# Two interleaved halves: another walk through the same elements in the gate operations of VectorE

## The chip, the core and the metric

The kernel runs on one core of one Trainium2 chip. The time is device microseconds (us) of one execution, from launch to end. A core has TensorE (PE, matrix products), VectorE (DVE), ScalarE (ACT), GpSimd (POOL) and SyncE (SP, which here issues the transfers, DMAs). Each engine works through its own list of instructions in a fixed order and waits at semaphores for the others.

## The reference

Two blocks follow each other. The first is a gated recurrence with complex decays, for 4 batches, 8 heads, 768 tokens and a head size of 48; the second is a two-layer network with a PReLU on 3072 tokens of 384 features, with 2048 hidden features.

```python
mag = np.sqrt(a_re * a_re + a_im * a_im)
scale = np.minimum(mag, 0.999) / (mag + 1e-06)
a_re_n, a_im_n = (a_re * scale, a_im * scale)
for t in range(S):
    ar, ai = (a_re_n[:, :, t, :, None], a_im_n[:, :, t, :, None])
    new_re = ar * S_re - ai * S_im
    new_im = ar * S_im + ai * S_re
    kv = np.einsum('bhd,bhe->bhde', k[:, :, t], v[:, :, t])
    S_re, S_im = (new_re + kv, new_im)
    y[:, :, t] = np.einsum('bhd,bhde->bhe', q[:, :, t], S_re)

x = y.transpose(0, 2, 1, 3).reshape(B * S, H * D)
h = x @ w_in
g = np.maximum(h, 0.0) + alpha * np.minimum(h, 0.0)
return g @ w_out
```

Everything is float32 on the chip.

## The kernel before, in words

**Stages.** The work is cut into tasks that are Python generators. `gates` (nine tasks, one per batch and group of C chunks of 128 tokens: one task with C=1, one with C=2, seven with C=3) loads the decays a_re and a_im, normalises them, forms products of the unit complex numbers along time and writes two scratch tensors to DRAM: `decs` (products of magnitudes) and `phs` (products of phases). `unit` (24 tasks, one per batch and chunk) loads q, k, v and those scratch tensors as the tiles KQ, V and VL, PP and T, and does the attention part of a chunk by levels: DVE multiplies KQ by phases (L742, L744) and by decays (L797), ACT copies parts of it (L820, L836), PE multiplies (L759), and masks, states and sums follow. `features` and `outputs` are the network: PE multiplies tokens by `w_in` (L978) into one of two PSUM buffers `ps_h`, ACT and DVE form the PReLU (L985, L987), PE multiplies by `w_out` (L997). For the last three groups of tokens `late_features` and `late_outputs` do the same with fewer products (L1097, L1172).

**Order.** A string, `ORDER`, says which task makes its next step; each step issues a few instructions. This one order fixes the list of every engine, so an instruction of `gates` on DVE stands between instructions of `unit` and of the network, and those behind it wait for it.

**The gate operations.** A gate task holds six areas of N = 3·128·C elements per partition (384, 768 or 1152) in one tile `gate`: x, c, f, d, e, y. For all tasks but the first, these DVE operations go over one whole area, in place: c+d (L269), e·c (L279), (e-3)·d (L281), c·d (L289), and x·d and y·d (L363, twice). The first task has its own lines (L305 to L323), in halves of 192. In all nine tasks `decays` forms the capped magnitude from c and f and writes it to `dec`, in rows of 128 with gaps of 128 (L380); a tree of products follows (L396). The chain of unit numbers uses `U`, which holds re and im as (m, n, i), that is the eight places within a block as four pairs, then the block n, then the place within the pair; products of neighbours go over it (L416, L418). The last step multiplies each block's numbers by the block's starting phase (L507, four per task) and sums (L510), and `phs` is written from there. The short recurrence over runs (L416 and L418 with 12 and 6 elements) is on DVE; other operations of up to 80 elements in the later gate tasks are on POOL.

In all of these the engines go through an area in the order in which it lies in memory, apart from L396, L416, L418 and L510, which take or leave pairs or every second element.

Of the kernel before, what the change touches and what calls it, by code (L numbers as in the profile page):

```python
# [14 lines left out]
ALU = mybir.AluOpType  # L15
# [3 lines left out]
P = 128  # L19
MAG_CAP = 0.999  # L20
# [4 lines left out]
GATE_SCALE = 2.0 ** 16  # L25
# [79 lines left out]
def kernel(  # L105
# [123 lines left out]
    def gates(g, b, c0, c1):  # L229
        C = c1 - c0  # L230
        n = C * P
        N = NK * n
        first, last = c0 == 0, c1 == NCH
        TT = nc.vector.tensor_tensor
        STT = nc.vector.scalar_tensor_tensor
# [11 lines left out]
        flat = flat_[:, 0:6 * N]  # L247
        G = flat.rearrange("p (r n) -> p r n", r=6)
        x, c, f, d, e, y = [G[:, i] for i in range(6)]
        dec = flat[:, 3 * N:5 * N].rearrange("p (m s) -> p m s", s=TL)  # L250
        for z, src in ((x, a_re), (y, a_im)):
            z = z.rearrange("p (t s) -> p t s", t=NK)
# [5 lines left out]
        if g:  # L258
            t = yield ACT(N, t)
            if last:  # L260
                ends_ = G[:, 0:6:5].rearrange("p r (t s) -> p r t s", t=NK)[:, :, :, n - 1]
                nc.scalar.activation(ends_, ident[:, 0:2 * NK].rearrange("p (r t) -> p r t", r=2), AF.Copy, scale=0.0)
            nc.scalar.activation(x, x, AF.Identity, scale=1.5, bias=bias_tiny)
            yield ACT(N)
            nc.scalar.activation(c, x, AF.Square, scale=GATE_SCALE)
            t = yield ACT(N, t)
            nc.scalar.activation(d, y, AF.Square, scale=1.5 * GATE_SCALE)
            t = yield DVE(N, t)
            TT(out=c, in0=c, in1=d, op=ALU.add)  # L269

            t = yield ACT(N, t)
            nc.scalar.activation(d, c, AF.Abs_reciprocal_sqrt)
            t = yield ACT(N, t)
            nc.scalar.activation(e, d, AF.Square)

            te = yield ACT(N, t)
            nc.scalar.activation(f, e, AF.Abs_reciprocal_sqrt)
            t = yield DVE(N, te)
            TT(out=e, in0=e, in1=c, op=ALU.mult)  # L279
            t = yield DVE(N, t)  # L280
            STT(out=d, in0=e, scalar=3.0, in1=d, op0=ALU.subtract, op1=ALU.mult)  # L281
            tf = yield ACT(N)
            nc.scalar.activation(f, f, AF.Square, scale=ONE / (1.5 * GATE_SCALE * MAG_EPS), bias=bias_one)
            tf = yield ACT(N)
            nc.scalar.activation(f, f, AF.Abs_reciprocal_sqrt)
            tf = yield ACT(N)
            nc.scalar.activation(f, f, AF.Identity, scale=ONE / 2.0, bias=bias_half)
            ts = yield DVE(N, t)
            TT(out=c, in0=c, in1=d, op=ALU.mult)  # L289
            ts = yield ACT(N, ts)  # L290
            nc.scalar.activation(c, c, AF.Copy, scale=1.0 / (1.5 * GATE_SCALE))
        else:
            parts = [[z[:, N // 2 * h:N // 2 * (h + 1)] for z in (x, c, f, d, e, y)] for h in range(2)]
            ready, tf, ts, txs = [None, None], [None, None], [None, None], [None, None]

            def enter(h):
                x, c, f, d, e, y = parts[h]
                yield ACT(N // 2, tx)
                nc.scalar.activation(x, x, AF.Identity, scale=1.5, bias=bias_tiny)
                yield ACT(N // 2)  # L300
                nc.scalar.activation(c, x, AF.Square, scale=GATE_SCALE)
                r = yield ACT(N // 2, t)
                nc.scalar.activation(d, y, AF.Square, scale=1.5 * GATE_SCALE)
                ready[h] = yield DVE(N // 2, r)
                TT(out=c, in0=c, in1=d, op=ALU.add)  # L305

            def root(h):
                x, c, f, d, e, y = parts[h]
                r = yield ACT(N // 2, ready[h])
                nc.scalar.activation(d, c, AF.Abs_reciprocal_sqrt)  # L310
                r = yield ACT(N // 2)
                nc.scalar.activation(e, d, AF.Square)
                r = yield ACT(N // 2)
                nc.scalar.activation(f, e, AF.Abs_reciprocal_sqrt)
                yield DVE(N // 2, r)
                TT(out=e, in0=e, in1=c, op=ALU.mult)
                yield DVE(N // 2)
                STT(out=d, in0=e, scalar=3.0, in1=d, op0=ALU.subtract, op1=ALU.mult)
                for p, w in ((y, -0.75), (x, -0.5)):
                    txs[h] = yield DVE(N // 2)  # L320
                    STT(out=p, in0=p, scalar=w * GATE_SCALE, in1=d, op0=ALU.mult, op1=ALU.mult)
                ts[h] = yield DVE(N // 2)
                TT(out=c, in0=c, in1=d, op=ALU.mult)  # L323

            for h in range(2):
                yield from enter(h)
            for h in range(2):
                yield from root(h)

        L = 8  # L330
        nb = N // L
        U = G[:, 0:3] if C > 2 else flat_[:, 6 * N:9 * N].rearrange("p (r n) -> p r n", r=3)
        U5 = U.rearrange("p r (m n i) -> p r m n i", m=L // 2, i=2)
# [7 lines left out]
        def by_place(z):  # L341
            return z.rearrange("p (n m i) -> p m n i", m=L // 2, i=2)

        def unit_numbers(*after):

            if not g:
                for h in range(2):
                    part = slice(nb // 2 * h, nb // 2 * (h + 1))
                    for o, p, by in ((2, y, 1.0), (0, y, -1.0), (1, x, 1.0)):
                        tu = yield ACT(N // 2, txs[h])  # L350
                        nc.scalar.activation(U5[:, o, :, part], by_place(p)[:, :, part], AF.Copy, scale=by)
                return tu
            for o, p in ((2, y), (1, x)):
                tu = yield ACT(N, tx, *after)
                nc.scalar.copy(U5[:, o], by_place(p))
            tu = yield ACT(N)
            nc.scalar.activation(U[:, 0], U[:, 2], AF.Copy, scale=-1.0)
            return tu

        if g:  # L360
            for p, w in ((x, -0.5), (y, -0.75)):
                tx = yield DVE(N, t)
                STT(out=p, in0=p, scalar=w * GATE_SCALE, in1=d, op0=ALU.mult, op1=ALU.mult)  # L363
        else:
            tu = yield from unit_numbers()
            tf = yield ACT(N)
            nc.scalar.activation(f, f, AF.Square, scale=ONE / (1.5 * GATE_SCALE * MAG_EPS), bias=bias_one)
            tf = yield ACT(N)
            nc.scalar.activation(f, f, AF.Abs_reciprocal_sqrt)
            tf = yield ACT(N)  # L370
            nc.scalar.activation(f, f, AF.Identity, scale=ONE / 2.0, bias=bias_half)
            ts = yield ACT(N, ts[1])
            nc.scalar.activation(c, c, AF.Copy, scale=1.0 / (1.5 * GATE_SCALE))
# [3 lines left out]
        def decays():  # L377

            t = yield DVE(N, ts, tf)
            STT(out=dec[:, :, 0:P], in0=c.rearrange("p (m s) -> p m s", s=P), scalar=-2.0 * MAG_CAP,  # L380
                in1=f.rearrange("p (m s) -> p m s", s=P), op0=ALU.max, op1=ALU.mult)
            yield POOL(2 * NK * C, t)
            nc.gpsimd.memset(dec[:, :, TL - 2:TL], 0.0)
            return t

        t = yield from decays()
        if C > 2:
            tu = yield from unit_numbers(t)
        f = y
        at = 0  # L390
        while at < TL - 4:
            m = (TL - at) // 2
# [28 lines left out]
        def turned(z, o):  # L421

            return z[:, 1 + o::-1][:, 0:2]
# [12 lines left out]
        off3 = y[:, 5 * nb:8 * nb].rearrange("p (r n) -> p r n", r=3)  # L436
# [37 lines left out]
        m = f[:, 0:2 * k].rearrange("p (a l n) -> p a l n", a=2, l=Rn - 1)  # L474
        for o in range(2):
            yield tiny(2 * k, t)
            tiny_engine.tensor_tensor(out=m, in0=blk[:, :, 0:Rn - 1],  # L477
               in1=turned(runs, o).unsqueeze(2).to_broadcast([P, 2, Rn - 1, rows]), op=ALU.mult)
# [24 lines left out]
        m = G[:, 3:5].rearrange("p a (m n i) -> p a m n i", m=L // 2, i=2)  # L503
        for o, p in enumerate((x, y)):
            for a in range(2):
                yield DVE(N, t, sent)
                TT(out=m[:, a], in0=U5[:, 1 + a], in1=turned(off3, o)[:, a].unsqueeze(1).unsqueeze(3).to_broadcast(  # L507
                    [P, L // 2, nb, 2]), op=ALU.mult)
            ts = yield DVE(N)
            TT(out=by_place(p), in0=m[:, 0], in1=m[:, 1], op=ALU.add)  # L510
            used = yield DMA(N / 2, ts)
            nc.sync.dma_start(phs[:, o, 1:n + 1].rearrange("(t p) s -> p t s", p=P), p.rearrange("p (t s) -> p t s", t=NK))
# [748 lines left out]
```

## Time and profile before

| what | value |
|---|---|
| median of three runs | 835.8 us (831.9 to 836.94) |
| the profiled execution | 834.89 us |
| its span, first to last instruction | 833.2 us |
| mean granted TensorE clock | 0.963 |
| PE busy | 685.4 us (82%) |
| DVE busy | 691.2 us (83%) in 1151 instructions |
| ACT busy | 502.7 us (60%) |
| POOL busy | 249.5 us (30%) |
| DMA moved | 130.98 MB |

The profile is of one execution. A row of the groups of instructions names the line, engine, operation, tiles and shapes; then the number of instructions, their busy time in us, the mean of one in ns, and the time that the engine sat idle just before them. A busy engine is not an engine at its peak: TensorE's ends are modelled. Shares are of the span. Times inside the profile are counted from the start of the span.

### The profile page before, as it was taken

Reading aid. Unit: us, or ns where it says so; the run is one execution under the profiler, and the core shown is the slowest. Engines: PE = TensorE matmul, PEld = TensorE weight load, DVE = VectorE, ACT = ScalarE, POOL = GpSimd, SP = SyncE. Lnnn points to the kernel's source line nnn. Section 1 sums busy time; section 2 is a strip of 40 time slices with the busy share of each in tenths; the row PEclk is TensorE's granted clock in tenths of the full one; section 3 lists DMA queues with packets and bytes.
Section 4 is the critical chain, followed back from the end, with each engine's and each line's share of the span. In section 5 each row is a group of like instructions: output and inputs, shape, how many; then the busy total and the mean of one; then the engine's idle time right before and its main releaser. Section 6 shows DMA issues by size and latency. Waiting matters only on the chain.

```text
span 833.2 us, 27790 instructions
## 1 busy us (share of the span) xinstructions
PE 685.4 (82%) x11680; PEld 542.5 (65%) x11680; DVE 691.2 (83%) x1151; ACT 502.7 (60%) x1243; POOL 249.5 (30%) x341
## 2 busy tenths in 40 slices
PE   0001316859999999899999999999999999999997
PEld 0001315646777667667777777776777777899997
DVE  6978989999999889899998999997887585556574
ACT  8848777557657767776876589554755645311121
POOL 7457454651503110233043121402300000323432
PEclk9999755979999999999999999999999999999999
DMA  7794885696678559547975779678476631201000
GB/s 210 224 274 121 251 233 163 194 217 162 154 226 195 149 145 261 152 123 214 247 177 156 233 165 208 179 193 189 96 204 146 158 90 36 61 2 39 1 20 20
DMA packets 186597, 130.98 MB, mean 157 GB/s; under 512 B 74728, under 2 KB 176872, under 8 KB 186088
## 3 DMA queue, kind: packets, MB, share of 16 engines
q1 hardware_dynamic: 186472, 129.20, 58.5%
q8 instruction: 92, 1.51, 0.8%
q14 instruction: 33, 0.27, 0.1%
HBM read 100.82 MB, written 35.71 MB: 164 GB/s over the span
## 4 chain that ended last, share of the span: by engine, by line
PE 62%; DMA 13%; DVE 11%; SPq 4%; ACT 4%; POOL 4%; issue 2%; DVEq 0%; ACTq 0%; POOLq 0%
PE ps_o L997 18%; PE ps_h L978 16%; PE ps_m L1172 6%; PE ps_lv L759 4%; PE ps_h L1097 3%; PE ps_y L1097 3%; PE ps_y L900 3%; PE ps_kv L880 2%; DVE KQ L797 2%; PE ps_y L930 2%; DVE gate L507 2%; DMA T<-decs 2%; DMA ysc<-T 2%; DMA VL<-in_v_dram 1%; DMA g_sb<-in_w_out_dram 1%
## 5 line engine op out<-in xcount | busy, mean ns | idle before, releaser
L978 PE MATMUL ps_h<-xT,w_in_sb 128*128 128x256 f32 (+1 forms) x960 | 227.8, 369 | 2.8 <-DMA xT<-ysc 1.8
L997 PE MATMUL ps_o<-w_out_sb,g_sb 128*128 128x384 f32 x576 | 224.7, 505 | 5.2 <-DVE g_sb L987 5.0
L978 PEld LDWEIGHTS ps_h<-xT,w_in_sb 128*128 128x128 f32 x960 | 173.0, 196 | 54.9 <-issue 3.2
L797 DVE TENSOR_TENSOR KQ<-KQ,T 96x1024 f32<-96x1024 f32 x120 | 148.8, 1241 | 25.4 <-PE ps_lv L759 18.1
L997 PEld LDWEIGHTS ps_o<-w_out_sb,g_sb 128*128 128x128 f32 x576 | 101.8, 191 | 45.6 <-DVE g_sb L987 7.6
L985 ACT ACTIVATE g_sb<-ps_h 128x256 f32<-128x256 f32 (+1 forms) x160 | 58.0, 362 | 84.7 <-PE ps_h L978 84.1
L759 PE MATMUL ps_lv<-WQ 96*32 96x32 f32 x2304 | 34.9, 204 | 81.7 <-DVE WQ L742 63.0
L416 POOL TENSOR_TENSOR gate<-gate 128x72 f32<-128x72 f32 (+1 forms) x56 | 43.1, 770 | 177.6 <-ACT gate L446 166.1
L759 PEld LDWEIGHTS ps_lv<-WQ 96*32 96x32 f32 x2304 | 26.6, 116 | 101.2 <-DVE WQ L742 63.4
L987 DVE SCALAR_TENSOR_TENSOR g_sb<-g_sb,al,ps_h 128x256 f32<-128x256 f32 (+1 forms) x160 | 71.4, 446 | 20.6 <-ACT g_sb L985 20.4
L1160 POOL TENSOR_TENSOR sums<-g_sb 128x128 f32<-128x128 f32 x48 | 21.9, 476 | 182.0 <-DMA VL<-in_v_dram 109.0
L916 ACT ACTIVATE St<-St,T 96x48 f32<-96x48 f32 x288 | 68.7, 325 | 6.1 <-DVE St L918 6.1
L820 ACT COPY WQ<-KQ 96x1024 f32<-96x1024 f32 x48 | 50.0, 1042 | 23.2 <-DVE KQ L797 23.2
L596 POOL TENSOR_SCALAR top<-top 128x768 f32<-128x768 f32 x16 | 42.6, 2668 | 28.4 <-ACT top L588 26.1
L900 PE MATMUL ps_y<-A,VL 64*48 64x64 f32 x2304 | 42.2, 222 | 8.3 <-issue 6.6
L477 POOL TENSOR_TENSOR gate<-gate,runs 128x252 f32<-128x252 f32 (+1 forms) x16 | 21.0, 1311 | 86.4 <-ACT runs L446 60.5
L507 DVE TENSOR_TENSOR gate<-gate 128x1152 f32<-128x1152 f32 (+2 forms) x36 | 44.3, 1263 | 2.9 <-POOL gate L492 2.7
L416 DVE TENSOR_TENSOR gate<-gate 128x576 f32<-128x576 f32 (+3 forms) x70 | 45.3, 647 | 1.3 <-ACT gate L446 0.4
L900 PEld LDWEIGHTS ps_y<-A,VL 64*48 64x48 f32 x2304 | 39.3, 123 | 10.4 <-issue 9.6
L836 ACT COPY W<-KQ 96x512 f32<-96x512 f32 x48 | 30.8, 642 | 23.7 <-DVE KQ L797 17.4
L759 PE MATMUL ps_lv<-KQ,W 96*32 96x32 f32 x1536 | 24.6, 205 | 24.3 <-ACT W L836 24.0
L773 ACT ACTIVATE A<-ps_lv,columns 128x64 f32<-128x64 f32 x144 | 37.7, 338 | 9.5 <-PE ps_lv L759 9.1
(169 smaller groups left out, 1365.3 us busy)
## 6 DMA issues: line engine op xcount, KB each, us to landing
T<-decs SPq DMA_DIRECT2D x48, 384.0 KB
PP<-phs SPq DMA_DIRECT2D x24, 387.0 KB
KQ<-in_q_dram SPq DMA_DIRECT2D x48, 192.0 KB
decs<-gate SPq DMA_DIRECT2D x7, 1152.0 KB
phs<-gate SPq DMA_DIRECT2D x14, 576.0 KB
KQ<-in_k_dram SPq DMA_DIRECT2D x40, 192.0 KB
vsc<-in_v_dram SPq DMA_DIRECT2D x48, 144.0 KB
VL<-vsc SPq DMA_DIRECT2D x48, 144.0 KB
```

The costliest lines, as they stand in the source:

```text
L416: on(4 * k).tensor_tensor(out=m, in0=w[:, 1::-1].unsqueeze(2).to_broadcast([P, 2, 2, k]), in1=pairs_of(u), op=ALU.mult)
L507: TT(out=m[:, a], in0=U5[:, 1 + a], in1=turned(off3, o)[:, a].unsqueeze(1).unsqueeze(3).to_broadcast([P, L // 2, nb, 2]), op=ALU.mult)
L759: nc.tensor.matmul(t[64 * i + j:64 * i + j + HC // 2, p], lhsT=keys(n, g), rhs=queries(n, g), start=True, stop=True)
L797: nc.vector.tensor_tensor(out=x, in0=x if x0 is None else x0, in1=m, op=ALU.mult)
L820: nc.scalar.copy(z.rearrange("p i n t -> p i (n t)").rearrange("p i (m h) -> p m i h", h=h), bass.AP(tensor=KQ.tensor, offset=KQ.offset + ...
L900: nc.tensor.matmul(o, lhsT=Vp[h][64 * i:64 * i + 64, s, e_ * D:(e_ + 1) * D], rhs=a, start=False, stop=False)
L916: nc.scalar.activation(St[:, n], before[:, n], AF.Copy, scale=T[0:D2, n, TL - 4 + s:TL - 3 + s])
L978: nc.tensor.matmul(p, lhsT=w_in_sb[:, f // 2, kk, f % 2 * P:(f % 2 + 1) * P], rhs=x_of[m][:, kk], start=(kk == 0), stop=(kk == NK - 1))
L985: nc.scalar.activation(gt, p, AF.Relu, scale=-1.0)
L987: nc.vector.scalar_tensor_tensor(out=gt, in0=gt, scalar=al_1[:, f:f + 1], in1=p, op0=ALU.mult, op1=ALU.add)
L997: nc.tensor.matmul(sums[0], lhsT=gt[:, c * P:(c + 1) * P], rhs=w_out_sb[:, f], start=(f == 0), stop=(f == NF - 1))
L1097: nc.tensor.matmul(o, lhsT=lhs, rhs=rhs, start=(at in (0, 5)), stop=(at in (4, 8)))
```

## The change

A helper reads an area of N elements as two halves and walks them in turn: element 0, element N/2, element 1, element N/2+1, and so on. It is put on all operands of L269, L279, L281, L289 and L363. In `decays` (L380) the walk goes across the 3·C rows of 128 first and along a row second. In L507 the block n is now the outer loop and the place of the pair the inner one; the two elements of a pair stay neighbours. What is computed and where it is stored stay as they are, the number of instructions too, and so does the order on every engine.

```diff
+        def strides(z):
+            return z.rearrange("p (a b) -> p b a", a=2)
+
...
             t = yield DVE(N, t)
-            TT(out=c, in0=c, in1=d, op=ALU.add)
+            TT(out=strides(c), in0=strides(c), in1=strides(d), op=ALU.add)
...
             t = yield DVE(N, te)
-            TT(out=e, in0=e, in1=c, op=ALU.mult)
+            TT(out=strides(e), in0=strides(e), in1=strides(c), op=ALU.mult)
             t = yield DVE(N, t)
-            STT(out=d, in0=e, scalar=3.0, in1=d, op0=ALU.subtract, op1=ALU.mult)
+            STT(out=strides(d), in0=strides(e), scalar=3.0, in1=strides(d), op0=ALU.subtract, op1=ALU.mult)
...
             ts = yield DVE(N, t)
-            TT(out=c, in0=c, in1=d, op=ALU.mult)
+            TT(out=strides(c), in0=strides(c), in1=strides(d), op=ALU.mult)
...
                 tx = yield DVE(N, t)
-                STT(out=p, in0=p, scalar=w * GATE_SCALE, in1=d, op0=ALU.mult, op1=ALU.mult)
+                STT(out=strides(p), in0=strides(p), scalar=w * GATE_SCALE, in1=strides(d), op0=ALU.mult, op1=ALU.mult)
...
             t = yield DVE(N, ts, tf)
-            STT(out=dec[:, :, 0:P], in0=c.rearrange("p (m s) -> p m s", s=P), scalar=-2.0 * MAG_CAP,
-                in1=f.rearrange("p (m s) -> p m s", s=P), op0=ALU.max, op1=ALU.mult)
+            STT(out=dec[:, :, 0:P].rearrange("p m s -> p s m"), in0=c.rearrange("p (m s) -> p s m", s=P), scalar=-2.0 * MAG_CAP,
+                in1=f.rearrange("p (m s) -> p s m", s=P), op0=ALU.max, op1=ALU.mult)
...
                 yield DVE(N, t, sent)
-                TT(out=m[:, a], in0=U5[:, 1 + a], in1=turned(off3, o)[:, a].unsqueeze(1).unsqueeze(3).to_broadcast(
-                    [P, L // 2, nb, 2]), op=ALU.mult)
+                TT(out=m[:, a].rearrange("p m n i -> p n m i"), in0=U5[:, 1 + a].rearrange("p m n i -> p n m i"),
+                   in1=turned(off3, o)[:, a].unsqueeze(2).unsqueeze(3).to_broadcast([P, nb, L // 2, 2]), op=ALU.mult)
```

## The prediction, made before the changed kernel ran

> **What bounds the kernel now.** I read the slices of the page first, then busy time by stretch, then the waits of PE and DVE, then single rows of DVE and ACT.
>
> In the slices (each digit is the busy share of 1/40 of the span, 20.8 us, in tenths):
>
> ```profile
> PE   0001316859999999899999999999999999999997
> DVE  6978989999999889899998999997887585556574
> ```
>
> The reader is to see two stages. Until about 190 us PE is half empty, and the chain of waits runs through transfers, POOL and DVE. From then on PE is full, and until about 600 us DVE is nearly full beside it.
>
> The same by stretches around the gate tasks. The columns are the stretch, its length, then busy us of PE, PE's weight loads, DVE, ACT and POOL, the granted clock, the DMA share and GB/s:
>
> ```profile
> 12.00:50.00 38.00, 0.00 (x0) 0.00 (x0) 35.09 (x89) 26.85 (x42) 16.74 (x17) 1.00 0.74 231
> 50.00:100.00 50.00, 12.42 (x396) 10.55 (x396) 41.62 (x56) 37.36 (x53) 34.76 (x29) 0.95 0.71 205
> 100.00:128.00 28.00, 5.55 (x140) 4.72 (x140) 23.17 (x26) 18.22 (x24) 14.70 (x15) 0.50 0.94 255
> ...
> 260.00:300.00 40.00, 37.96 (x642) 28.04 (x635) 35.18 (x52) 30.05 (x78) 13.41 (x22) 0.96 0.56 138
> ...
> 330.00:370.00 40.00, 36.14 (x724) 26.61 (x723) 37.06 (x58) 30.23 (x79) 10.73 (x15) 1.00 0.61 157
> ...
> 408.00:440.00 32.00, 30.79 (x651) 23.29 (x650) 30.18 (x38) 26.67 (x69) 10.36 (x15) 1.00 0.79 194
> ...
> 484.00:514.00 30.00, 30.00 (x588) 22.66 (x590) 28.52 (x40) 25.77 (x70) 8.71 (x15) 1.00 0.76 179
> ```
>
> DVE has 38.00 - 35.09 = 2.9 us to spare in the first of these, then 8.4, 4.8, 4.8, 2.9, 1.8 and 1.5. In the waits of 200 to 514 us, PE waits for nothing in particular for more than a few us, and most of DVE's idle time there is put down to PE (ps_lv) or to ACT behind PE (g_sb). Two engines that are this full hand work to each other through two ps_h buffers: a delay of DVE is soon one of PE, and PE has no gap in which to make it up.
>
> **The change, part by part.** The built lists of instructions of the two kernels agree on every engine in number and order; only access patterns differ, L269 for instance being 384x2 instead of 768. So nothing is removed, added or moved, no queue is passed, no transfer and no wait is new. What can change is the duration of 57 DVE operations that now take each element from another place than the one before, and of the 36 of L507.
>
> Elements per partition that hop: six operations (L269, L279, L281, L289, twice L363) in seven tasks of 1152 and one of 768 make 6 × (7 × 1152 + 768) = 52,992. L380 adds 7 × 1152 + 768 + 384 = 9,216. Together 62,208.
>
> What a hop costs, the trace of before doesn't show for a long DVE operation. The nearest rows, here of DVE and ACT (the number after the bar's busy time is the mean of one in ns):
>
> ```profile
> L363 DVE SCALAR_TENSOR_TENSOR gate<-gate 128x1152 f32<-128x1152 f32 x14 | 19.0, 1368 | 0.0
> L510 DVE TENSOR_TENSOR gate<-gate 128x1152 f32<-128x1152 f32 x14 | 19.0, 1355 | 0.2
> L744 DVE TENSOR_TENSOR KQ<-KQ,PP 96x1024 f32<-96x1024 f32 x24 | 30.0, 1249 | 0.1
> L416 DVE TENSOR_TENSOR gate<-run,runs 128x12 f32<-128x12 f32 x48 | 8.2, 171 | 0.8
> L396 DVE TENSOR_TENSOR gate<-gate 128x12 f32<-128x12 f32 x1 | 0.2, 171 | 0.0
> L480 DVE TENSOR_TENSOR gate<-gate 128x42 f32<-128x42 f32 x1 | 0.2, 236 | 0.0
> L488 DVE TENSOR_TENSOR gate<-gate 128x48 f32<-128x48 f32 x1 | 0.2, 208 | 0.0
> L444 ACT COPY gate<-gate 128x288 f32<-128x288 f32 x7 | 5.0, 710 | 4.3 <-DVE gate L418 4.3
> L486 ACT ACTIVATE gate<-gate 128x288 f32<-128x288 f32 x7 | 3.1, 440 | 6.7 <-POOL gate L480 6.7
> ```
>
> - No cost: L744 steps 8 bytes on all three operands and L510 writes pairs with gaps between them; both go at the rate of L363, which is contiguous (1249 for 1024 and 1368 for 1152 differ by 0.93 ns per element). L416 on 12 elements reads in steps of some 28 bytes and takes the 171 ns of L396; 12 elements would show only 10 ns.
> - A cost: L480 writes 42 single elements 32 bytes apart. L488 writes 48 neighbours in 208 ns; at about 1.04 ns each (1368 - 171 over 1152 - 12 is 1.05) 42 would take 202, so each hop cost (236 - 202) / 42 = 0.81 ns. One sample, with POOL beside it. On ACT, L444 writes single elements 72 bytes apart and L486 as many neighbours: (710 - 440) / 288 = 0.94 ns.
>
> The bounds are thus 0 (the 28-byte reads) and, if reads and writes each pay as a write does here, 2 × 0.85 = 1.7 ns; below 0 nothing in these rows points. I take 0.85, between the DVE row and the ACT row and nearer to the first: the changed operations write single elements 2304 bytes apart (L380: 1024), which is nearest to L480. An operation of 1152 goes from 1360 to 1360 + 0.98 us = 2.34 us; DVE gains 62,208 × 0.85 ns = 52.9 us.
>
> The Trainium skill, page "Vector Engine (DVE) Microarchitecture Reference", section "Measured stream behaviour on trn2", speaks against the change: a port keeps its rate only in runs of two or more adjacent words, and with all three operands hopping it lists 1.98 ns per column against 1.054. By that an estimate of 0.93 × 62,208 = 57.6 us would stand for the 52.9. For words 8 bytes apart L744 does not bear the rule out in that form.
>
> L507 I cost at nothing: its pairs stay together on both long operands, as in L510, and only the repeated phase is read in another order.
>
> **What of it shows at the end.** A task of 1152 adds 6.85 us to DVE, the task of 768 4.6, the first 0.3. Lower end: each stretch uses all the idle time that it has. Then 4.9 - 2.9 = 2.0 remain in 12 to 50 us, nothing in 50 to 100, 2.0 in 100 to 128, 1.7 around the task of 182 to 213 (5.2 us idle in 170 to 260), 2.0 in 260 to 300, 3.9 in 330 to 370, 5.0 in 408 to 440, 5.4 in 484 to 514: 22 us. Upper end: all 52.9. Against the lower end speaks that DVE's waits are for PE and ACT, which come later themselves when DVE does, and that POOL, on the chain from 49 to 63 us, is held up beside DVE's operations of two operands:
>
> ```profile
> 52.44 0.29 POOL L416 TENSOR_TENSOR gate<-gate 128x48 f32<-128x48 f32 x1
> ...
> 54.04 2.50 POOL L416 TENSOR_TENSOR gate<-gate 128x48 f32<-128x48 f32 x1
> ```
>
> (DVE ran L744 and L269 back to back then.) Against the upper end speaks the second ps_h buffer, with which PE runs on for a group of some 2 us, and the transfers that carry the chain from 99 to 127 us. I take the middle, 37.5 us. The profiled execution is 834.9 us (span 833.2, 1.7 around it), 0.9 below the median of 835.8: 834.9 + 37.5 = **872 us**.
>
> **Rivals.**
> 1. The halves cost nothing because two alternating streams are each still sequential and both places are kept at hand; only L380, with nine rows in turn, pays. DVE gains 9,216 × 0.85 = 7.8 us, and by the same share of the way between the ends (0.7) 5.5 us show: 840. For it: the reads of L416 at no cost; against: L480 and L444 write regular steps too, and pay. The same section of the Trainium skill reports one stream alternating between two regions at the full read rate, for an operation with one source; no run here shows that yet.
> 2. Not slower: no hop costs anything at such lengths, because an operation over 1152 elements has its next ones fetched well ahead; L480's 34 ns are then POOL's doing and ACT's price is ACT's own. DVE's rows stay at 1350 to 1390 and the time is that of before, 832 to 838. It decides if the hop's price is under 0.15 ns, where the 9 us that it adds to DVE vanish in its 32 us of idle time in the stretches above. A faster end would need the interleaved operations to free POOL; no row shows such a thing.
> 3. Reads and writes both pay: 1.7 ns. DVE gains 106 us, more than all its idle time from 12 to 514 us (43 us), so between 63 and 106 show: about 920.
> 4. The change does nothing because the walk is straightened out again when the kernel is built; the 384x2 in the built list speaks against that. It would look like 2 and is counted there.
>
> **How the numbers follow.** Forecast 0.70: 834.9 plus 22 to 53, that is 857 to 888, and with a price of 0.65 to 1.0 ns 852 to 897. Rival 1 0.12 (836 to 846), rivals 2 and 4 0.08, rival 3 0.08, anything faster 0.02. The range of 840 to 897 holds the forecast's 0.70 and most of rival 1. A measurement tells about 1% from no change here. Over 1% slower: forecast, rival 3 and a fifth of rival 1, 0.80; within 1%: the rest of rival 1 and most of rival 2, 0.16; faster 0.04.
>
> **What would show it.** Right: L269 to L363 and L380 at about 2.3 us, L507 near 1.39, DVE busy near 691 + 53 = 744, PE's work unchanged with new waits for DVE from 200 to 514 us, and from 600 us on the same tail, shifted. Step by step: a price other than 0.85 shows in those rows; a share other than 0.7 in the span against DVE's gain. Wrong: the long rows at 1.35 us (rival 2), only L380 longer (rival 1), L507 longer by more than 0.1 us, or a span that grows by more than DVE's busy time, which POOL's waits would then have to explain.

## The result, and the profile after

The changed kernel takes 888.55 us in the median (886.87 to 889.81, four runs) beside 834.33 us of the kernel before (four runs, one more than in the table above): a ratio of 1.0648, with a 95% interval of 1.0606 to 1.069. The profiled execution took 889.81 us, its span is 888.1 us, 54.9 more than before.

The top of the page after, busy time of each engine and the slices:

```profile
PE 696.1 (78%) x11680; PEld 547.9 (62%) x11680; DVE 741.3 (83%) x1151; ACT 505.4 (57%) x1243; POOL 309.4 (35%) x341
...
PE   0001302976799989988998999799999999999998
...
POOL 7467559436050340064053406240220000223433
```

DVE gained 50.1 us in the same number of instructions. PE's work is 1.6% longer, at a mean granted clock of 0.948 instead of 0.963, and its digits between 200 and 600 us now have holes (7, 8). And POOL, which the change doesn't touch, gained 59.9 us (249.5 before). The span gained more than DVE did.

The shares of the chain of waits, before and then after:

```profile
PE 62%; DMA 13%; DVE 11%; SPq 4%; ACT 4%; POOL 4%; issue 2%; DVEq 0%; ACTq 0%; POOLq 0%
```

```profile
PE 44%; DVE 24%; POOL 12%; DMA 7%; ACT 5%; issue 4%; SPq 2%; DVEq 0%; POOLq 0%; ACTq 0%
```

DVE had 11% and POOL 4% of it before, and 24% and 12% after, so both are now on the way to the end for longer.

The groups of instructions after (line, engine, operation, shapes, number, then busy us, mean ns, idle before), in the order of the lines shown before; L367, L384, L511 and L514 are L363, L380, L507 and L510 of before:

```profile
L367 DVE SCALAR_TENSOR_TENSOR gate<-gate 128x1152 f32<-128x1152 f32 x14 | 32.5, 2343 | 0.0
...
L384 DVE SCALAR_TENSOR_TENSOR gate<-gate 128x1152 f32<-128x1152 f32 x7 | 18.3, 2620 | 0.0
...
L511 DVE TENSOR_TENSOR gate<-gate 128x1152 f32<-128x1152 f32 x28 | 38.0, 1387 | 0.1
L514 DVE TENSOR_TENSOR gate<-gate 128x1152 f32<-128x1152 f32 x14 | 19.0, 1355 | 0.2
```

The walk in halves went from 1.37 to 2.34 us, the decays' operation from 1.37 to 2.62 us. The phase products, whose pairs stay together, did not move. The gains of all hopping rows add up to 55 us; DVE's busy time gained less, since a hopping operation overlaps the one behind it for longer: in the timeline shown further down, L293 starts at 80.09, lasts 2.34, and the next starts at 82.28, an overlap of 0.15 us, where the contiguous L801 before it overlaps by 0.07. Over 57 operations 0.08 us more make the difference.

### The profile page after: what moved, and what is told of

Its sections match the earlier page's. It is cut to its first block, busy times and chain, and to the rows that moved or that the text cites. A ratio compares the mean times of both kernels' runs of the same rounds, so it can differ in the third digit from the quotient of the medians.

```text
span 888.1 us, 27790 instructions
## 1 busy us (share of the span) xinstructions
PE 696.1 (78%) x11680; PEld 547.9 (62%) x11680; DVE 741.3 (83%) x1151; ACT 505.4 (57%) x1243; POOL 309.4 (35%) x341
## 4 chain that ended last, share of the span: by engine, by line
PE 44%; DVE 24%; POOL 12%; DMA 7%; ACT 5%; issue 4%; SPq 2%; DVEq 0%; POOLq 0%; ACTq 0%
PE ps_o L1001 11%; PE ps_h L982 11%; PE ps_m L1176 6%; DVE KQ L801 5%; POOL gate L422 5%; PE ps_h L1101 3%; PE ps_y L1101 3%; PE ps_lv L763 3%; DVE gate L511 3%; DMA T<-decs 2%; POOL gate L420 2%; PE ps_y L904 2%; PE ps_kv L884 2%; DVE g_sb L991 2%; DVE gate L514 2%
## 5 line engine op out<-in xcount | busy, mean ns | idle before, releaser
L1001 PE MATMUL ps_o<-w_out_sb,g_sb 128*128 128x384 f32 x576 | 227.4, 510 | 12.1 <-DVE g_sb L991 9.7
L982 PE MATMUL ps_h<-xT,w_in_sb 128*128 128x256 f32 (+1 forms) x960 | 230.3, 373 | 1.3 <-DVE g_sb L991 1.3
L982 PEld LDWEIGHTS ps_h<-xT,w_in_sb 128*128 128x128 f32 x960 | 175.0, 198 | 54.5 <-issue 3.3
L801 DVE TENSOR_TENSOR KQ<-KQ,T 96x1024 f32<-96x1024 f32 x120 | 148.2, 1236 | 19.8 <-PE ps_lv L763 13.5
L420 POOL TENSOR_TENSOR gate<-gate 128x72 f32<-128x72 f32 (+1 forms) x56 | 51.1, 913 | 175.3 <-ACT gate L450 163.8
L824 ACT COPY WQ<-KQ 96x1024 f32<-96x1024 f32 x48 | 50.1, 1044 | 27.9 <-DVE KQ L801 27.5
L600 POOL TENSOR_SCALAR top<-top 128x768 f32<-128x768 f32 x16 | 53.3, 3338 | 28.2 <-ACT top L592 28.2
L422 POOL TENSOR_TENSOR gate<-gate 128x36 f32<-128x36 f32 (+1 forms) x56 | 58.3, 1040 | 4.2
L420 DVE TENSOR_TENSOR gate<-gate 128x576 f32<-128x576 f32 (+3 forms) x70 | 46.4, 664 | 0.9
L511 DVE TENSOR_TENSOR gate<-gate 128x1152 f32<-128x1152 f32 (+2 forms) x36 | 44.3, 1263 | 3.3 <-POOL gate L496 3.1
L872 PE MATMUL ps_kt<-ident,KQ 96*128 96x96 f32 x192 | 26.7, 265 | 26.0 <-ACT T L875 21.3
```

What stands on the lines that cost most here:

```text
L420: on(4 * k).tensor_tensor(out=m, in0=w[:, 1::-1].unsqueeze(2).to_broadcast([P, 2, 2, k]), in1=pairs_of(u), op=ALU.mult)
L422: on(2 * k).tensor_tensor(out=dst, in0=m[:, 0], in1=m[:, 1], op=ALU.add)
L511: TT(out=m[:, a].rearrange("p m n i -> p n m i"), in0=U5[:, 1 + a].rearrange("p m n i -> p n m i"), in1=turned(off3, o)[:, a].unsqueeze(2) ...
L600: nc.gpsimd.tensor_scalar(out=top, in0=top, scalar1=F64_SMALL, scalar2=None, op0=ALU.max)
L801: nc.vector.tensor_tensor(out=x, in0=x if x0 is None else x0, in1=m, op=ALU.mult)
L982: nc.tensor.matmul(p, lhsT=w_in_sb[:, f // 2, kk, f % 2 * P:(f % 2 + 1) * P], rhs=x_of[m][:, kk], start=(kk == 0), stop=(kk == NK - 1))
```

## The experiments

The theory after the result had two parts: the hops cost DVE what the rows say, and the end moves by more than DVE's gain because POOL is held up beside it. Gains below are those of the profiled execution against that of before (DVE 691.2, POOL 249.5, span 833.2); ratios are those of the timed runs. The median of before differs by up to 4.7 us from chip to chip, so a quotient of gains of some 50 us is good to about 0.1, and one of some 16 us to about 0.3.

### One part of the change at a time

`halves_only` keeps the six operations in halves; the decays' operation and the phase products are those of before.

```diff
-            STT(out=dec[:, :, 0:P].rearrange("p m s -> p s m"), in0=c.rearrange("p (m s) -> p s m", s=P), scalar=-2.0 * MAG_CAP,
+            STT(out=dec[:, :, 0:P], in0=c.rearrange("p (m s) -> p m s", s=P), scalar=-2.0 * MAG_CAP,
...
-                TT(out=m[:, a].rearrange("p m n i -> p n m i"), in0=U5[:, 1 + a].rearrange("p m n i -> p n m i"),
+                TT(out=m[:, a], in0=U5[:, 1 + a], in1=turned(off3, o)[:, a].unsqueeze(1).unsqueeze(3).to_broadcast(
```

> Only the walk in halves (six operations per gate task but the first) is kept; the operation on the decays and the phase products are as before. Theory A (each hopping operation costs VectorE its longer time, and the end moves by a little more than VectorE's gain because both engines are full and GpSimd is held up too): VectorE gains about 41 us of its 50, the time goes to 834 + 45 = 879 (ratio 1.054). Rival B (the share of 0.7 of the prediction holds and something else in the change gives the rest): 834 + 29 = 863 (1.035). Rival C (the halves are nearly free, the decays' nine rows pay): under 842.

Measured: ratio 1.0543 (1.0489 to 1.0597), DVE +40.0 us, POOL +56.6, span +48.5. Theory A's 1.054 was met. Most of the change is here, and nearly all of what POOL gained.

`decays_only` changes L380 alone in the kernel before, as the change does.

> Only the operation on the decays walks across its rows. Theory A: nine instructions, 2.6 instead of 1.37 us for the seven long ones, VectorE gains 9 us, the time 10 us: 844 (1.012). Rival B: 0.7 of it, 840.5 (1.008). Rival C: the operation is the last one of its chain, the tree of products and the transfer of the decays wait for it, so it costs more than its length: over 850 (1.02).

Measured: 1.0117 (1.007 to 1.0163), DVE +13.2 (10.1 of it in L380's rows), POOL +8.8, span +5.2 in the profiled execution, the fastest of its six. Theory A's value; the 1.008 of B lies in the interval too, and C is out: the operation costs about its length although others wait for it.

`phase_only` changes L507 alone.

> Only the order of the phase products is changed. Theory A: their rows stay at 1.387 us, as in the profile after, and the time stays: 834 (0.997 to 1.003). Rival: the order of the repeated operand hinders GpSimd beside it although VectorE's own time stays: 838 or more (1.005).

Measured: 1.0024 (0.9992 to 1.0056), and L507 stays at 1367 ns. Its cost can't be told from nothing.

### What a hop costs, by itself

`prices` puts nine additions of the same 1152 elements, each with another walk, behind the third gate operation of the seven long tasks, where `e` is dead:

```diff
+            if C > 2:
+                TT(out=e, in0=c, in1=d, op=ALU.add)
+                TT(out=e, in0=halved(c), in1=d, op=ALU.add)
+                TT(out=e, in0=halved(c), in1=halved(d), op=ALU.add)
+                TT(out=halved(e), in0=c, in1=d, op=ALU.add)
+                TT(out=halved(e), in0=halved(c), in1=halved(d), op=ALU.add)
+                TT(out=paired(e), in0=paired(c), in1=paired(d), op=ALU.add)
+                TT(out=rows9(e), in0=rows9(c), in1=rows9(d), op=ALU.add)
+                TT(out=eighths(e), in0=c, in1=d, op=ALU.add)
+                TT(out=e, in0=eighths(c), in1=eighths(d), op=ALU.add)
```

`paired` walks the halves two elements at a time, `rows9` goes across the rows of 128 as the decays do, `eighths` steps 32 bytes.

> The kernel before with nine more two-operand additions of 1152 elements after the third gate operation of each task with three chunks, into an area that is dead there; its own time (about 834 + 140) says nothing, the rows do. Contiguous 1.35 us. Theory A (each port pays for single elements far apart, but reads and writes overlap): halves on one source 2.1, on both 2.1, on the result alone 2.1, on all three 2.35, pairs kept together on all three 1.36, nine rows 2.6, results 32 bytes apart 2.3 (the 0.81 ns of the prediction), sources 32 bytes apart 2.3. Rival B (two alternating streams of reads are free, the write pays everything): halves on sources 1.35, on the result alone 2.35. Rival C (price per operand adds up): 1.7, 2.0, 1.7 and 2.35.

The single lines' instructions of this kernel give the least, the median and the greatest of seven durations in ns; the lines follow the order of the diff:

```profile
L295 DVE TENSOR_TENSOR gate<-gate x7: 1357/1359/1558, 72.8 to 605.0; 128x1152 f32<-128x1152 f32 x7
L296 DVE TENSOR_TENSOR gate<-gate x7: 1378/1384/1420, 74.4 to 606.4; 128x1152 f32<-128x1152 f32 x7
L297 DVE TENSOR_TENSOR gate<-gate x7: 1370/1383/1561, 75.8 to 607.8; 128x1152 f32<-128x1152 f32 x7
L298 DVE TENSOR_TENSOR gate<-gate x7: 2156/2162/2211, 77.4 to 609.2; 128x1152 f32<-128x1152 f32 x7
L299 DVE TENSOR_TENSOR gate<-gate x7: 2310/2319/2326, 79.7 to 611.4; 128x1152 f32<-128x1152 f32 x7
L300 DVE TENSOR_TENSOR gate<-gate x7: 1358/1359/1360, 82.0 to 613.8; 128x1152 f32<-128x1152 f32 x7
L301 DVE TENSOR_TENSOR gate<-gate x7: 2552/2627/2631, 83.4 to 615.2; 128x1152 f32<-128x1152 f32 x7
L302 DVE TENSOR_TENSOR gate<-gate x7: 2228/2230/2237, 86.1 to 617.8; 128x1152 f32<-128x1152 f32 x7
L303 DVE TENSOR_TENSOR gate<-gate x7: 2224/2224/2599, 88.3 to 620.0; 128x1152 f32<-128x1152 f32 x7
```

Against the first line: reading one or both sources in halves costs (1384 - 1359) / 1152 = 0.02 ns per element, nearly nothing. Writing in halves costs (2162 - 1359) / 1152 = 0.70, all three 0.83; so sources in halves add (2319 - 2162) / 1152 = 0.14 once the result hops too. Two elements at a time cost nothing. Nine rows in turn cost 1.10, steps of 32 bytes 0.76 for the result and 0.75 for the sources. So theory A was close on every row but the two with sources alone in halves, where rival B was right; B's 2.35 for the result alone was too much, and its free reads do not hold for steps of 32 bytes. C met only the row with all three in halves.

### Extra work without hops

`extra_two` leaves every operation contiguous and adds short contiguous additions of two operands behind each of the 57, with the durations meant to add what the hops add; `extra_one` adds sums over one operand instead.

```diff
+    def extra(pieces, k, x, y, z):
+        for i in range(pieces):
+            nc.vector.tensor_tensor(out=more[:, 0:k], in0=x[:, i * k:i * k + k], in1=y[:, i * k:i * k + k], op=ALU.add)
...
             TT(out=c, in0=c, in1=d, op=ALU.add)
+            extra({1152: 3, 768: 2}[N], 240, c, d, c)
```

> The kernel before, all operations contiguous, with more work on VectorE behind each of the 57 operations that the change made longer: contiguous additions of two SBUF operands in pieces of 240 elements (229 and 187 behind the decays) into a small spare area, as long together as the hops' cost in the profile after (0.98, 0.65 and 1.25 us). Theory A (only VectorE's time counts, and GpSimd being held up beside two-operand work): VectorE +50 us, time +50 to +58: 884 to 892 (1.06 to 1.07). Rival D (a hopping operation holds GpSimd up by being one long instruction; pieces let it in): VectorE +50, GpSimd near its 250 us, time +35 to +45: 869 to 879.

> The same pieces as sums over one contiguous operand instead of additions of two. Theory A1 (GpSimd is held up by VectorE's operations of two operands only, and that makes the end move by more than VectorE's gain): VectorE +50 us, GpSimd stays near 250 us instead of 309, time +35 to +42: 870 to 876 (1.043 to 1.05). Theory A2 (VectorE is the bound by itself and GpSimd's waiting is beside the point): time as with two operands, 884 or more.

Measured: with two operands 1.0632 (1.0558 to 1.0705), DVE +69.0, POOL -0.2, span +56.3. With one operand 1.0565 (1.0492 to 1.0638), DVE +61.2, POOL +2.0, span +51.1. The pieces cost more than I had reckoned, 440 and 403 ns each, so the times don't compare with the change directly. Per microsecond of DVE's gain the span moved by 56.3 / 69.0 = 0.82 and 51.1 / 61.2 = 0.83, and by 54.9 / 50.1 = 1.10 with the change. POOL's busy time stayed in both, as rival D and theory A1 had expected, and so did the share of about 0.8. But A1's ground fell with that: in pieces, two operands are no worse for POOL than one. The mean granted clock of `extra_two` is 0.948 and PE's busy time 697.1 us, as with the change; so TensorE's pace is not what sets 0.82 and 1.10 apart.

### Early and late tasks

`early` hops in the first four gate tasks only, `late` in the last five, by a condition in the helper and in `decays`:

```diff
-            return z.rearrange("p (a b) -> p b a", a=2)
+            return z.rearrange("p (a b) -> p b a", a=2) if g < 4 else z
```

> Hops in the first four gate tasks only (they end at 128 us in the profile before); the phase products as before. VectorE gains (0.2 + 4.5 + 2 x 7.0) x 0.91 = 17 us. The prediction's stretches: 2.0 + 0 + 2.0 of these at least, 4 us: 838 (1.005). Theory A (idle time of VectorE in this stage is no room, since the chain goes through GpSimd and VectorE in turn): 17 to 20 us: 851 to 854 (1.02 to 1.024).

> Hops in the last five gate tasks only (from 182 us). VectorE gains 5 x 7.0 x 0.91 = 32 us. The prediction's stretches: 1.7 + 2.0 + 3.9 + 5.0 + 5.4 = 18 us at least, 852 (1.022). Theory A: 32 to 38 us: 866 to 872 (1.038 to 1.046). If early and late add up to the whole change, the two stages don't hide each other's delay.

Measured: early 1.026 (1.0185 to 1.0336), DVE +16.0, POOL +24.6, span +21.1. Late 1.0352 (1.0268 to 1.0436), DVE +32.7, POOL +39.5, span +33.8. Together 1.061, the whole change within the intervals: the stages don't hide each other's delay. Per microsecond of DVE's gain the early tasks cost 1.32 and the late 1.03. The early time is that of theory A; the late one lies between the prediction's stretches (1.022, outside the interval) and the lower end of A (1.038, inside it). The prediction's lower end for the early stretches, 4 us, was far off, though DVE had 16 us idle there.

### Is it the hop, or the long instruction, that holds POOL up?

`extra_whole` adds the contiguous work in one piece each, written to dead parts of the gate's area; the pieces came out at 1.1 us, longer than meant.

```diff
+        more = {1152: 874, 768: 544}.get(N)
+
+        def extra(k, o, p, q):
+            TT(out=o[:, 0:k], in0=p[:, 0:k], in1=q[:, 0:k], op=ALU.add)
...
             TT(out=c, in0=c, in1=d, op=ALU.add)
+            extra(more, e, c, d)
```

`hops_pieces` cuts each hopping operation of the changed kernel in two, `hops_four` in four; `after_again` is the changed kernel once more, on the chip of `hops_four`.

```diff
-            TT(out=strides(c), in0=strides(c), in1=strides(d), op=ALU.add)
+            for half in (slice(0, N // 4), slice(N // 4, N // 2)):
+                TT(out=strides(c)[:, half], in0=strides(c)[:, half], in1=strides(d)[:, half], op=ALU.add)
```

> As the extra additions of two operands in pieces, but each in one piece (874 elements, 544 in the task of 768, 1132 behind the decays), so each about 0.99 us long; written where the gate's area is dead, for which the one of the third operation waits until after the fourth. VectorE +50 us. Theory H (a hopping operation, not a long one, keeps GpSimd out: the pieces, 19 us more on VectorE than the change, left GpSimd at 249 us): GpSimd stays within 245 to 262 us, the time moves by 0.8 of VectorE's gain, +40: 876 (1.048). Rival L (any run of long two-operand instructions keeps GpSimd out, pieces let it in): GpSimd 290 us or more, time +50 to +55: 886 to 891 (1.06 to 1.066).

> The changed kernel with each hopping operation cut in two (576 elements each, 1.25 us, as short as the contiguous ones of before; the operation on the decays in two halves of its rows). VectorE gains 50 + 57 x 0.08 = 54 us. Theory H: GpSimd stays at 300 us or more, time +55 to +62: 890 to 897 (1.066 to 1.074). Rival L: GpSimd gets in between, 250 to 275 us, time +40 to +48 in spite of the additional instructions: 876 to 883 (1.048 to 1.057).

> The changed kernel once more, beside the next one on the same chip. 1.0648 before; every theory expects 1.061 to 1.069, VectorE 741, GpSimd 305 to 313 us.

> The changed kernel with each hopping operation cut in four (288 elements, 0.7 us each). Cut in two, VectorE's busy time was that of the changed kernel (741.0), GpSimd's 294.5 instead of 309.4, and the ratio 1.0538. Theory M (GpSimd gets its turn between VectorE's two-operand instructions, and later the longer they are; this is what moves the end by more than VectorE's own gain): GpSimd 265 to 285 us, and the time moves by 0.8 to 0.9 of VectorE's gain (about 741 to 750 busy, +50 to +59), so 1.048 to 1.06, under the changed kernel. Rival V (the gain by cutting in two was the chip's or chance, GpSimd's waiting is beside the point): 1.065 or more, since there are 171 instructions more than in the changed kernel.

Measured, with the changed kernel's first profile on top:

| kernel | DVE gain, us | POOL gain, us | span gain, us | span per DVE gain | ratio (95%) |
|---|---|---|---|---|---|
| the change | 50.1 | 59.9 | 54.9 | 1.10 | 1.0648 (1.0606 to 1.069) |
| `after_again` | 50.1 | 59.8 | 53.7 | 1.07 | 1.0604 (1.0548 to 1.0659) |
| `hops_pieces` | 49.8 | 45.0 | 44.2 | 0.89 | 1.0538 (1.0482 to 1.0593) |
| `hops_four` | 51.8 | 11.1 | 39.6 | 0.76 | 1.0436 (1.0405 to 1.0468) |
| `extra_whole` | 59.3 | 25.6 | 45.2 | 0.76 | 1.057 (1.0515 to 1.0624) |

`extra_whole` stood between the two theories (POOL 275.1; H expected up to 262, L from 290), and `hops_pieces` did too (294.5, but the time of L). So neither holds alone. `after_again` came out just under the 1.061 expected. `hops_four` settled the direction: with DVE's busy time within 2 us, POOL's falls with the length of the pieces and the time falls with it, on one chip from 1.0604 to 1.0436, although 171 instructions are added. Both fell further than theory M had said (POOL 260.6, expected 265 to 285; ratio from 1.048). Rival V is out.

How POOL waits can be seen on a single operation. It is L480 in the second gate task; in the tasks behind the first, L477, L480, L488 and L492 are on POOL whatever their size, so also with more than 80 elements. Before, with start and duration in us, first POOL, then the next DVE operation that waited for POOL:

```profile
72.14 4.98 POOL L480 TENSOR_TENSOR gate<-gate 128x84 f32<-128x84 f32 x1
```

```profile
81.08 2.44 DVE L507 TENSOR_TENSOR gate<-gate 128x768 f32<-128x768 f32 x2 [2.75 <-POOL gate L492]
```

The same operation after, and what DVE did meanwhile:

```profile
79.10 8.91 POOL L484 TENSOR_TENSOR gate<-gate 128x84 f32<-128x84 f32 x1
```

```profile
78.96 1.20 DVE L801 TENSOR_TENSOR KQ<-KQ,T 96x1024 f32<-96x1024 f32 x1
80.09 2.34 DVE L293 TENSOR_TENSOR gate<-gate 128x1152 f32<-128x1152 f32 x1
82.28 1.20 DVE L801 TENSOR_TENSOR KQ<-KQ,T 96x1024 f32<-96x1024 f32 x1
83.41 4.49 DVE L367 SCALAR_TENSOR_TENSOR gate<-gate 128x1152 f32<-128x1152 f32 x2
90.98 1.57 DVE L511 TENSOR_TENSOR gate<-gate 128x768 f32<-128x768 f32 x1 [3.09 <-POOL gate L496]
```

In `hops_four` POOL came to it earlier, beside the pieces of L288 (L281 of before); the second POOL line is an operation that follows soon after:

```profile
75.08 1.91 POOL L490 TENSOR_TENSOR gate<-gate 128x84 f32<-128x84 f32 x1
...
80.62 6.12 POOL L498 TENSOR_TENSOR gate<-gate 128x96 f32<-128x96 f32 x1 [1.45 <-ACT gate L496]
```

```profile
75.14 2.37 DVE L288 SCALAR_TENSOR_TENSOR gate<-gate 128x288 f32<-128x288 f32 x4
```

And in `hops_pieces`:

```profile
77.02 10.98 POOL L490 TENSOR_TENSOR gate<-gate 128x84 f32<-128x84 f32 x1
```

Before and after, POOL starts beside the same DVE operation (L797, L801 after), the first of the same five with two operands in SBUF that follow each other without a gap. Before, POOL is through at 77.12, while the fifth still runs; after, only at 88.01, when DVE, at 87.9, has run out of them. The Trainium skill, page "SBUF — State Buffer", section "Who interferes with whom", says that a VectorE instruction with two SBUF inputs contends with a GpSimd instruction that reads SBUF. The 8.91 us agree, and go beyond one instruction's length: POOL waited through five. Pieces help on the whole, but not each time: in `hops_pieces` the same operation took 10.98 us, and the 6.12 us in `hops_four` last until DVE is through with the eight pieces of L372 at 86.6.

This wait hardly reached the end: DVE's idle time behind it is 3.09 us, and was 2.75 before. The wait that does is in the last gate task. There POOL multiplies and adds in L416 and L418 (L420 and L422 after), and ACT copies the outcome in L444 (L448 after). Before, POOL and ACT:

```profile
502.80 0.26 POOL L418 TENSOR_TENSOR gate<-gate 128x36 f32<-128x36 f32 x1
```

```profile
508.58 0.24 ACT L444 COPY runs<-gate 128x36 f32<-128x36 f32 x1
```

After, POOL, ACT, PE and DVE:

```profile
551.74 9.19 POOL L422 TENSOR_TENSOR gate<-gate 128x36 f32<-128x36 f32 x1
```

```profile
561.69 0.22 ACT L448 COPY runs<-gate 128x36 f32<-128x36 f32 x1 [6.59 <-POOL gate L422]
```

```profile
563.24 0.90 PE L872 MATMUL ps_kt<-ident,KQ 96*128 96x96 f32 x4 [6.14 <-ACT T L875]
```

```profile
563.61 0.48 DVE L991 SCALAR_TENSOR_TENSOR g_sb<-g_sb,al,ps_h 128x256 f32<-128x256 f32 x1 [2.78 <-ACT g_sb L989]
```

Before, POOL is done some 5 us ahead of ACT's copy. After, ACT stands 6.59 us for POOL, and behind the copy in ACT's list stand the copies out of `ps_kt` and the first half of the PReLU, `g_sb`, for which PE and DVE wait: PE stands 6.14 us and DVE 2.78. So POOL's waiting comes to the end through ACT. All idle time of ACT that the traces put down to POOL adds up to 15.5 us before, 39.8 after, 37.1 in `after_again`, 31.0 in `hops_pieces`, 17.4 in `hops_four` and 17.9 in `extra_whole`, the order of the shares in the table. In `extra_two` and `extra_one`, with shares of 0.82 and 0.83, it is 13.1 and 15.0. `early` and `late`, with 22.8 and 31.6 and shares of 1.32 and 1.03, stand the other way round; the share of `early` is uncertain, and there may be another way to the end.

## Why the prediction came out right, and where it was off

The time was forecast at 872, with 840 to 897 as the range; it is 888.55. That the range holds it is in part luck: with the price of 0.85 ns the forecast went up to 888, where all of DVE's gain shows. What lies above stood there for a price of up to 1.0 ns, and DVE gained less than forecast, not more. One of the prediction's own signs of being wrong came out, a span that grows by more than DVE's busy time, "which POOL's waits would then have to explain"; they do.

- **The count of hops** and that nothing else moves: right. The instructions are as many as before, PE's busy time is 1.6% longer by the trace, and the last 233 us are the old tail shifted (PE busy 228.1 us in it, 228.2 before).
- **The price of a hop, 0.85 ns**: right in size. L363's line gives (2343 - 1368) / 1152 = 0.85; the decays' line 1.09, which the prediction had at 0.85 too. DVE's gain was forecast at 52.9 and is 50.1 us. What it rested on, L480's 42 single writes at 0.81, is close to `prices`' 0.76 for that step, which was luck in part: it came from 34 ns of a single operation, and L480's other one on DVE took 735 ns. The reason that the prediction gave weight to, single elements written far apart, holds: 0.70 of the 0.83 in `prices` is the write's. Halves on the sources alone cost 0.02, and 0.14 on top of the write.
- **L507 at nothing**: right (1387 before and after; `phase_only` 1.0024).
- **What of it shows, 37.5 of 52.9 us, a share of 0.7**: this is the term that was mis-sized. It was 54.9 of 50.1. Where POOL is let in, the share is 0.76 (`hops_four`) or 0.82 (`extra_two`), not far from 0.7. The rest, 886.9 - 872.8 = 14.1 us of span on one chip between the whole hops and those in four pieces, goes with POOL's waiting, which holds up ACT, and through ACT PE and DVE (the 6.59, 6.14 and 2.78 us above). The prediction named POOL's wait as a reason against its lower end and gave it no price, so that the time passed its upper end, all of DVE's gain. It also took idle time of DVE in the early stretches as room; `early` shows that it was none.
- **The low end for a price of 0.65 ns**, 852, is the 22 us scaled down. By the prediction's own rule, idle time taken off each stretch, it would be about 846; nothing hangs on it.
- **Rival 1** (halves free, decays pay): the reads by themselves bear out its mechanism, the write does not; `halves_only` at 1.0543 rules its time out. What the Trainium skill, page "Vector Engine (DVE) Microarchitecture Reference", section "Measured stream behaviour on trn2", reports of a one-source operation, one stream that alternates between two regions at the full rate, agrees with the two sources here, at 0.02 ns. The table of that section in the Trainium skill has 1.76 ns per column for both sources hopping, and no run here shows that for two halves: 1383 ns for 1152 elements. The 1.98 there for all three operands, 0.93 above contiguous, is near the 0.83 of `prices`.
- **Rivals 2 to 4**: the rows, 2.34 us for the halves, rule out both a free hop and a price of 1.7.

What stays open: how POOL's turn is decided. Cut in shorter pieces, the hops hold it up less in total, but `extra_whole` and `hops_pieces`, with pieces of similar length (1.1 and 1.25 us), held it up by 25.6 and 45.0 us. The longest POOL operation took 3.77 us in the one and 10.98 in the other, beside 5.75 before and 11.03 after. That points to the hop itself as a second cause, but no run tests it at equal length. Whether the contiguous kernel would gain from gate operations in shorter pieces wasn't tried.

## What to carry to other kernels

Walk at least two neighbouring elements at a time on all operands of a VectorE operation: the interleaved halves were free then. Single results from two halves, in steps of 32 bytes or across nine rows cost 0.7 to 1.1 ns per float32 element here, and single sources in steps of 32 bytes as much. Where GpSimd works on SBUF beside VectorE, the price of a longer two-operand operation is its own length and what others then wait for GpSimd; so look at GpSimd's rows and at the waits for it, not at VectorE's alone. Cutting such operations in four returned about a quarter of the loss here (14.3 of 50.8 us on one chip).

## What the runs showed of the hardware that I hadn't expected

- Sources read alternately from two places 2304 bytes apart run nearly at the contiguous rate (1384 against 1359 ns for 1152 elements); the alternate write pays (2162). Steps of 32 bytes cost the sources as much as the result (2224 and 2230).
- A hopping operation cut in four costs hardly more of DVE's time than whole: DVE's busy time was 743.0 against 741.3 us with 171 more instructions.
- One GpSimd operation on 84 elements can wait through five VectorE instructions, 8.91 us. Cut in pieces, these let it through in 1.91 us once and kept it for 10.98 another time.
- A GpSimd operation of 36 elements that took 9.19 us instead of 0.26 kept TensorE idle for 6.14 us, by way of one short copy in ScalarE's list.
